# A spectral mixing and state-space kernel on one core: the first input tile in one transfer, a fourth staging buffer, and one constant that borrows another's place

## The chip, the cores and the metric

The kernel runs on one core of a Trainium2 chip. The metric is the device time of the whole program in microseconds; lower is better. The engines are named as in the profile: PE is the matrix multiplier and PEld its weight loads, DVE the vector engine, ACT the scalar (activation) engine, POOL the general one, and SP the engine whose queue issues nearly all transfers.

## The reference

Two independent branches, side by side in the output (2048 x 1024, single precision). Branch A is a Fourier mixing layer written as matrix products, branch B a long convolution with a kernel made from state-space parameters, here with the same length L = 2048 and width D = 512.

```
# branch A: real part of a DFT along the hidden and the sequence axis
a = einsum("bsd,ed->bse", x, dft_hid_re);  b = einsum("bsd,ed->bse", x, dft_hid_im)
yA = einsum("ts,bse->bte", dft_seq_re, a) - einsum("ts,bse->bte", dft_seq_im, b)
# branch B
dt = exp(log_dt);  A = -exp(log_A_real) + 1j*A_imag;  C = (C_real + 1j*C_imag)*dt
K  = 2 * Re( sum_n C[d,n] * exp(A[d,n]*dt[d]*l) )          # [D, L]
yB = irfft( rfft(u, 2L) * rfft(K, 2L) )[:L] + u * D_skip
out = concatenate([yA, yB], -1)
```

## The kernel before

**Branch A** (class `Fnet`) does the sequence transform first. For four column blocks t and the two parts c (cosine, sine) it forms x^T times a 512-column block of the sequence matrix: eight "s" groups of 16 k steps, whose results p go to DRAM. Then four "p" groups of 8 k steps multiply them with the hidden matrix. Each single-precision operand is split into a rounded `hi` (ACT, L212) and a remainder `lo` (DVE, L216), and a product is three matmuls: hi by hi, hi by lo, lo by hi (L333). A k step is four output blocks d of three matmuls each, 128 x 128 by 128 x 512, so twelve; there are 1,920 in all. The stationary x tiles are loaded once, into `x_raw`, four slots of a buffer that branch B uses later (`uk`). The moving tiles (sT, later p) come through four `raw` buffers and three `hi`/`lo` pairs.

A group's four PSUM banks are evacuated by ACT into `y` buffers (`evacuate`, L359) and stored from there by SP (L364 to p, L367 to the output). There are three y buffers (`STAGED`); a y is free again when its store has landed. The last block of the last group uses two of them, one half copied by ACT (L353), the other by DVE (L354).

**Branch B** (class `Ssm`) builds the kernel's taps from tables (DVE, ACT; L575, L584, L591), multiplies them on PE (L771), and runs a two-stage transform: stage one of u (`stage1_u`, L846, with the constant `f1u`) and of the taps (L801, `f1k`), each stored to DRAM (xu, L862; xk); stage two (`product`, L926, with `w2`, loads L899), the product on DVE, and two inverse stages (L961 with `ia`, L1007 in `inverse`, with `ib`, which loads `zl` tiles at L1002). The constants come in two sets (`constants`, L440): f1u, f1k and dskip early, then w2, ia and ib.

**Order.** The order on every engine's queue is made when the program is built. A list scheduler (`Plan`) runs each piece as a generator that asks for an engine with an estimated time (`yield "pe", 0.685, None, 6`: engine, microseconds, urgency, instructions) or waits for an event or a buffer (`Sem`). Of the pieces that could start first, the more urgent one is taken, and its instructions go to the engine's queue at that point; the engine then works strictly in that order. Branch A's matmuls have the lowest rank on PE, so they fill what branch B leaves. The number of y buffers enters as `self.ys = Sem(STAGED)`.

**The start.** The first x tile is loaded in two transfers: the first 128 columns alone (`load_x0`, L247), then the other 384 (`load_x1`, L259). The first sT tile leaves at the same time through ACT's queue (L296). While these travel, PE multiplies zeros (`warm`, L232: seven matmuls, which are 14 instructions in the profile); one more zero matmul stands behind the first three real matmuls.

Of the kernel before, what the change touches and what calls it, by code (L numbers as in the profile page):

```python
# [8 lines left out]
F32 = mybir.dt.float32  # L9
# [47 lines left out]
class Sem:  # L57


    def __init__(self, n):  # L60
        self.free, self.waiting = [0.0] * n, []
# [109 lines left out]
def act(cols):  # L171
    return 0.09 + cols * 0.00085


def dve(cols, rate=1.0):
    return (62 + cols / rate) / 960


def load(kb):
    return max(0.55, kb / 330)  # L180


class Fnet:
# [40 lines left out]

    def warm(self):

        yield "pe", 3.1, None, 28
        self.zeros(7)

    def zeros(self, n):  # L230
        for _ in range(n):
# [11 lines left out]

    def load_x0(self, raw):

        yield "dma", load(64)
        self.nc.sync.dma_start(raw[:, :128], self.xin[0, :, :128])  # L247
        self.x[0] = self.still(0)
        yield "act", act(128)
        self.nc.scalar.activation(self.x[0][0][:, :128], raw[:, :128], AF.Copy)  # L250
        yield "dve", dve(128)
        self.nc.vector.tensor_tensor(self.x[0][1][:, :128], raw[:, :128], self.x[0][0][:, :128].bitcast(F32),
                                     op=OP.subtract)
        self.plan.set(self.x0_ev)

    def load_x1(self, b, raw, n):
        cols = slice(0 if n else 128, DM)
        yield "dma", load(256)
        self.nc.sync.dma_start(raw[:, cols], self.xin[n, :, cols])  # L259
        if n:  # L260
            self.x[n] = self.still(n)
        else:
            yield self.hi_ev
        yield from self.split(*(a[:, cols] for a in self.x[n]), raw[:, cols])
        self.plan.set(self.x_ev[n])
        self.x_left -= 1
        if not self.x_left:
            self.plan.put(b.uks)
# [42 lines left out]
    def matmuls(self):  # L311
        nc = self.nc
        for g in self.groups:
            still = (self.x, self.x_ev) if g[0] == "s" else (self.w, self.w_ev)
            items, acc = self.items[g], []
            for batch in [[i] for i in items[:-BATCH]] + [items[-BATCH:]]:
                for d in range(4):
                    if batch[0][3] == 0:
                        yield self.acc
                        acc.append(self.psum.tile([128, DM], F32, name="acc"))  # L320
                    for i in batch:
                        k = i[3]
                        yield self.m_ev[i]
                        yield still[1][k] if k or d or g != self.groups[0] else self.x0_ev
                        (shi, slo), (mhi, mlo) = still[0][k], self.m[i]
                        first = i == self.items[self.groups[0]][0] and not d
                        yield "pe", 0.685, None, 10 if first else 6
                        cols = slice(128 * d, 128 * d + 128)
                        three = (shi, mhi), (shi, mlo), (slo, mhi)
                        if still[1][k] is self.x_ev[0] and not d:  # L330
                            three = three[::2] + three[1:2]
                        for n, (l, r) in enumerate(three):
                            nc.tensor.matmul(acc[d], l[:, cols], r, start=k == 0 and n == 0,  # L333
                                             stop=k == len(items) - 1 and n == 2)
                        if first:
                            self.zeros(1)
                        if d == 3:
                            self.plan.put(self.ss)
                            self.split_ahead -= 1
                            if i[:3] == ("s", 3, 1) and k < 8:  # L340
                                self.plan.set(self.x_free[k])
                    if batch[-1] is items[-1]:
                        self.plan.spawn(self.evacuate(g, d, acc[d]), -1)
# [54 lines left out]
class Ssm:  # L398


    def __init__(self, tc, ctx, plan, nd, ldt, dsk, uG, f1u, f1k, w2, ia, ib, out):
        self.tc, self.nc, self.plan = tc, tc.nc, plan
        self.nd, self.ldt, self.uG, self.out = nd, ldt, uG, out
        self.const = ctx.enter_context(tc.tile_pool(name="b_const", bufs=1))
        self.fps = ctx.enter_context(tc.tile_pool(name="b_fps", bufs=1, space=PSUM))
        dram = ctx.enter_context(tc.tile_pool(name="b_dram", bufs=1, space=DRAM))
        self.xu = dram.tile([64, 2, 32, DM], F32, name="xu")
        self.xk, self.zs = (dram.tile([4, 64, 2, 32, PART], F32, name=n) for n in ("xk", "zs"))
        self.dt_dram = dram.tile([128, 4], F32, name="dt_dram")
        self.par_dram = dram.tile([128, 4, DM - FIRST], F32, name="par_dram")  # L410
        first = ("f1u", f1u), ("f1k", f1k), ("dskip", dsk)
        second = ("w2", w2), ("ia", ia), ("ib", ib)
        self.cst = [[(n, self.const.tile([128, *a.shape[1:]], F32, name=n), a) for n, a in s] for s in (first, second)]
        self.halfpi = self.const.tile([128, 1], F32, name="halfpi")
        self.slots, self.fs, self.one = [0, 1], Sem(2), Sem(1)
        self.t1s, self.t2s, self.css = Sem(2), Sem(1), Sem(2)
        self.kss, self.res, self.xks = Sem(1), Sem(1), Sem(1)
        self.waiting, self.taps_left, self.pars = [], 16, Sem(1)
        self.sets, self.set_ev = {}, [Event(), Event()]
        self.const_ev, self.const2_ev, self.xu_ev = Event(), Event(), Event()  # L420
        self.xk_ev, self.zs_ev = [Event() for _ in range(4)], [Event() for _ in range(4)]

    def set_buffers(self, i, pool):
# [436 lines left out]
    def store_u(self, x, m, sem):  # L860
        yield "dma", load(512)
        self.nc.sync.dma_start(self.xu.rearrange("s c l d -> (s c) l d")[:, 2 * m:2 * m + 2], x)  # L862
        self.plan.put(sem)
        self.uleft -= 1
        if not self.uleft:
            self.plan.put(self.sets[0].zls)
            self.plan.set(self.xu_ev)

# [127 lines left out]
    def inverse(self, b, h, i, n):  # L996

        nc = self.nc
        z = b.pool.tile([128, n, PART], F32, name="zl", bufs=b.n)
        yield "dma", load(64 * n)  # L1000
        for o in range(0, n, 8):
            nc.sync.dma_start(z[:, o:o + 8], self.zs[h].rearrange("s c l d -> (s c) l d")[:, n * i + o:n * i + o + 8])  # L1002
        (k, ps), = yield from self.banks(1)
        yield "pe", 0.1 + 0.1025 * n, None, 4 * n + 1
        for w in range(n // 2):
            for y in range(2):
                nc.tensor.matmul(ps[64 * y:64 * y + 64, w // 4, PART * (w % 4):PART * (w % 4) + PART],  # L1007
                                 self.ib[:, n * i + 2 * w + y], z[:, 2 * w + y], start=True, stop=True,
                                 tile_position=(0, 64 * y))
        o = n * i // 2  # L1010
        for w in range(0, n // 2, 4):
            yield "act", act(512)
            nc.scalar.activation(z[:, w:w + 4], ps[:, w // 4].rearrange("p (w d) -> p w d", w=4), AF.Copy)
        self.give(k)
        yield "dma", load(32 * n)
        nc.sync.dma_start(self.out[:, o:o + n // 2, PART * h:PART * h + PART], z[:, :n // 2])
        self.plan.put(b.zls)


CHUNK, FIRST = 32, 128  # L1020
RAWS, DEPTH, STAGED, AHEAD = 4, 3, 3, 3
BATCH = 2


# [70 lines left out]
```

## Time and profile before

| | before |
|---|---|
| timed runs, us | 590.11, 591.39, 592.93 (median 591.39) |
| profiled execution, us | 589.94 |
| its span, first to last instruction, us | 588.1 |
| PE, DVE, ACT busy, us | 581.5, 494.3, 381.0 |
| granted PE clock | 1.00 |
| data moved, MB | 125.84 |

Busy time of PE is the time in which at least one matmul is under way; matmuls overlap, so a busy PE can still be slower than it could be. The time of the profiled execution is 1.84 us longer than its span. In timeline rows the columns are start, duration, engine, line, operation and tiles; idle time before the row and what ended it stand in brackets.

### The profile page before, as it was taken

The page shows a single profiled execution, that of the slowest core. Times are in us where ns is not written, and L with a number is a line of the kernel's source. Part 1 is how long each engine was busy: PE and PEld are TensorE (multiplying, and loading weights), DVE is VectorE, ACT ScalarE, POOL GpSimd, SP SyncE. Part 2 cuts the span into 40 slices and gives each one's busy share as a digit, 9 for nine tenths or more (in the row PEclk, how much of TensorE's full clock was granted, in tenths as well). Part 3 has the DMA queues.
Part 4 walks back from the last instruction along what each step waited for, and adds up shares of the span by engine and source line. Part 5 has one row for each costly group of instructions (what it writes and reads, how often), then busy time and mean ns, then how long its engine had stood idle before and what let it go on. Part 6 is the DMA issues. An engine that isn't in the chain of part 4 may idle for free.

```text
span 588.1 us, 14925 instructions
## 1 busy us (share of the span) xinstructions
PE 581.5 (99%) x5968; PEld 441.9 (75%) x5968; DVE 494.3 (84%) x883; ACT 381.0 (65%) x745; POOL 4.8 (1%) x12
## 2 busy tenths in 40 slices
PE   9999999999999999999999999999999999999997
PEld 7767668778778767877787778777877777777785
DVE  6986989999999999999999999999999944254320
ACT  5789884946676767758584866678755536264532
POOL 0000000000000000000000000000000000000000
PEclk9999999999999999999999999999999999999999
DMA  7999996363494369446768594568798845998574
GB/s 264 324 356 320 350 334 220 98 198 79 118 270 111 93 178 265 136 128 167 231 204 244 152 276 129 150 169 258 237 289 215 256 111 163 316 325 266 158 260 144
DMA packets 141238, 125.84 MB, mean 214 GB/s; under 512 B 46192, under 2 KB 106352, under 8 KB 140912
## 3 DMA queue, kind: packets, MB, share of 16 engines
q1 hardware_dynamic: 140880, 124.48, 69.8%
q8 instruction: 47, 0.77, 0.6%
q10 hardware_dynamic: 288, 0.39, 0.2%
q14 instruction: 23, 0.19, 0.1%
HBM read 82.12 MB, written 42.73 MB: 212 GB/s over the span
## 4 chain that ended last, share of the span: by engine, by line
PE 69%; DVE 14%; DMA 7%; ACT 4%; issue 3%; SPq 2%; DVEq 0%; ACTq 0%
PE acc L333 52%; PE f L926 5%; PE f L771 4%; DVE prod L575 4%; DVE lo L216 3%; PE f L961 3%; PE f L1007 3%; DVE t L584 2%; DMA xt<-xk 2%; PE f L801 2%; DMA raw<-in_sT 2%; SPq L899 1%; DMA uk<-in_x 1%; DMA xu<-z 1%; DMA cs<-in_ldt 1%
## 5 line engine op out<-in xcount | busy, mean ns | idle before, releaser
L333 PE MATMUL acc<-hi,x_hi 128*128 128x512 f32 x640 | 257.5, 402 | 0.5 <-ACT x_hi L212 0.2
L333 PE MATMUL acc<-lo,x_hi 128*128 128x512 f32 x640 | 250.0, 391 | 0.2 <-DVE lo L216 0.2
L333 PE MATMUL acc<-hi,x_lo 128*128 128x512 f32 x640 | 249.8, 390 | 0.1
L575 DVE TENSOR_TENSOR prod<-t,cs 128x1024 f32<-128x1024 f32 (+4 forms) x192 | 163.9, 870 | 3.5 <-ACT t L713 1.4
L216 DVE TENSOR_TENSOR lo<-raw,hi 128x512 fp32r<-128x512 f32 x160 | 109.1, 686 | 61.7 <-ACT hi L212 61.7
L333 PEld LDWEIGHTS acc<-hi,x_hi 128*128 128x128 f32 x640 | 120.2, 188 | 48.7 <-issue 20.8
L212 ACT ACTIVATE hi<-raw 128x512 fp32r<-128x512 f32 x160 | 100.2, 628 | 82.3 <-PE acc L333 63.5
L333 PEld LDWEIGHTS acc<-hi,x_lo 128*128 128x128 f32 x640 | 120.3, 188 | 26.5 <-DVE x_lo L216 0.5
L333 PEld LDWEIGHTS acc<-lo,x_hi 128*128 128x128 f32 x640 | 120.4, 188 | 23.8 <-DVE lo L216 0.8
L584 DVE TENSOR_TENSOR t<-prod 128x512 f32<-128x512 f32 (+4 forms) x192 | 94.1, 512 | 1.0
L591 ACT ACTIVATE square<-t 128x256 f32<-128x256 f32 (+1 forms) x64 | 36.7, 573 | 30.0 <-DVE t L584 28.1
L359 ACT ACTIVATE y<-acc 128x512 f32<-128x512 f32 x47 | 27.9, 597 | 11.7 <-PE acc L333 8.4
L771 PEld LDWEIGHTS f<-t,t 128*32 128x32 f32 x2048 | 29.5, 110 | 6.4 <-issue 3.8
L938 ACT ACTIVATE uk<-f 128x1024 f32<-128x1024 f32 x32 | 31.9, 1013 | 3.7 <-PE f L926 3.7
L926 PE MATMUL f<-xt,w 64*32 64x256 f32 x1024 | 31.9, 379 | 0.6 <-DMA xt<-xk 0.5
L771 PE MATMUL f<-t,t 128*32 128x64 f32 x2048 | 32.2, 220 | 0.3 <-issue 0.3
L941 DVE TENSOR_TENSOR z<-uk 128x512 f32<-128x512 f32 x32 | 22.0, 687 | 6.8 <-ACT uk L938 6.8
L926 PEld LDWEIGHTS f<-xt,w 64*32 64x32 f32 x1024 | 18.6, 106 | 11.9 <-issue 3.7
L650 ACT ACTIVATE cs<-cs 128x352 f32<-128x352 f32 x32 | 16.1, 538 | 14.2 <-DVE cs L645 14.2
L604 DVE TENSOR_TENSOR t<-square 128x128 f32<-128x128 f32 (+1 forms) x64 | 24.7, 386 | 0.0
L976 ACT ACTIVATE z<-f 128x512 f32<-128x512 f32 x32 | 17.5, 596 | 10.2 <-PE f L771 5.1
L598 DVE SCALAR_TENSOR_TENSOR t<-t 128x128 f32<-128x128 f32 (+2 forms) x48 | 22.4, 466 | 0.3
(81 smaller groups left out, 411.5 us busy)
## 6 DMA issues: line engine op xcount, KB each, us to landing
raw<-in_sT SPq DMA_DIRECT2D x127, 256.0 KB, 3.7
p<-y SPq DMA_DIRECT2D x32, 256.0 KB, 4.2
xt<-xu SPq DMA_DIRECT2D x32, 256.0 KB, 4.8
xk<-xk_sb SPq DMA_DIRECT2D x32, 256.0 KB, 4.0
xt<-xk SPq DMA_DIRECT2D x32, 256.0 KB, 5.4
zs<-z SPq DMA_DIRECT2D x32, 256.0 KB, 3.7
zl<-zs SPq DMA_DIRECT2D x16, 512.0 KB, 6.4
raw<-p SPq DMA_DIRECT2D x32, 256.0 KB, 4.0
```

The lines of the kernel that those rows point to most:

```text
L212: self.nc.scalar.activation(hi, src, AF.Copy)
L216: self.nc.vector.tensor_tensor(lo, src, hi.bitcast(F32), op=OP.subtract)
L333: nc.tensor.matmul(acc[d], l[:, cols], r, start=k == 0 and n == 0, stop=k == len(items) - 1 and n == 2)
L359: self.nc.scalar.activation(y, ps, AF.Copy, scale=-1.0 if g[2] == 1 else 1.0)
L575: self.nc.vector.tensor_tensor(p.rearrange("p k d c m -> p k (d c) m"), src.rearrange("p d c l -> p (d c) l")[:, None, :, rows].to_broadca ...
L584: self.nc.vector.tensor_tensor(dst[:, :, :, rows], p[:, 0], p[:, 1, :, ::-1], op=OP.add)
L591: self.nc.scalar.activation(sq, t[:, :, :, m // 2:m], AF.Square)
L598: self.nc.vector.scalar_tensor_tensor(t[:, :, 1, m:2 * m:2], t[:, :, 0, m // 2:m], 2.0, t[:, :, 1, m // 2:m], op0=OP.mult, op1=OP.mult)
L604: self.nc.vector.tensor_tensor(t[:, :, 0, m:2 * m:2], box[0][:, :, 0], box[0][:, :, 1], op=OP.subtract)
L771: nc.tensor.matmul(ps[32 * j:32 * j + 32, i], t1[:, d, c], t2[:, d, c], start=c == 0, stop=c == 1, tile_position=(0, 32 * j))
L926: nc.tensor.matmul(both[:, :, c], self.w2[rows, 2 * q + r, xx, 32 * c:32 * c + 32], xt[rows, r, xx], start=True, stop=True, tile_position= ...
L938: a.activation(uk[:, r].rearrange("p g n c d -> p g (n c d)"), p, AF.Copy)
```

## The change

Three things change. (1) The first x tile comes in one transfer of 256 KB; `load_x1` no longer issues one for it, but ACT and DVE still split the first 128 columns ahead of the others. The scheduler is told 440 KB for this one transfer. (2) All eight zero matmuls stand ahead of the first real one, none behind it. (3) There are four y buffers instead of three. `f1u` has no place of its own: it lies in the first 128 columns of `ib`, and `ib` is loaded only when the last store of u's first stage has been scheduled (`const3_ev`); `inverse` waits for that before it loads its `zl`.

```diff
     def warm(self):
-        yield "pe", 3.1, None, 28
-        self.zeros(7)
+        yield "pe", 3.5, None, 32
+        self.zeros(8)
...
     def load_x0(self, raw):
-        yield "dma", load(64)
-        self.nc.sync.dma_start(raw[:, :128], self.xin[0, :, :128])
+        yield "dma", load(440)
+        self.nc.sync.dma_start(raw, self.xin[0])
         self.x[0] = self.still(0)
...
     def load_x1(self, b, raw, n):
         cols = slice(0 if n else 128, DM)
-        yield "dma", load(256)
-        self.nc.sync.dma_start(raw[:, cols], self.xin[n, :, cols])
         if n:
+            yield "dma", load(256)
+            self.nc.sync.dma_start(raw, self.xin[n])
             self.x[n] = self.still(n)
         else:
             yield self.hi_ev
...
                         (shi, slo), (mhi, mlo) = still[0][k], self.m[i]
-                        first = i == self.items[self.groups[0]][0] and not d
-                        yield "pe", 0.685, None, 10 if first else 6
+                        yield "pe", 0.685, None, 6
...
-                        if first:
-                            self.zeros(1)
...
-        first = ("f1u", f1u), ("f1k", f1k), ("dskip", dsk)
-        second = ("w2", w2), ("ia", ia), ("ib", ib)
-        self.cst = [[(n, self.const.tile([128, *a.shape[1:]], F32, name=n), a) for n, a in s] for s in (first, second)]
+        constants = ("f1u", f1u), ("f1k", f1k), ("dskip", dsk), ("w2", w2), ("ia", ia), ("ib", ib)
+        t = {n: self.const.tile([128, *a.shape[1:]], F32, name=n) for n, a in constants[1:]}
+        t["f1u"] = t["ib"][:, :2].rearrange("p l y -> p (l y)")
+        cst = [(n, t[n], a) for n, a in constants]
+        self.cst = cst[:3], cst[3:5], cst[5:]
...
         self.uleft -= 1
         if not self.uleft:
+            self.plan.spawn(self.constants(2, self.const3_ev), 3)
             self.plan.put(self.sets[0].zls)
             self.plan.set(self.xu_ev)
...
         z = b.pool.tile([128, n, PART], F32, name="zl", bufs=b.n)
+        yield self.const3_ev
         yield "dma", load(64 * n)
...
-RAWS, DEPTH, STAGED, AHEAD = 4, 3, 3, 3
+RAWS, DEPTH, STAGED, AHEAD = 4, 3, 4, 3
```

More of the change, by code (lines that the diff above doesn't have):

```diff
@@ L419, in __init__ @@
         self.sets, self.set_ev = {}, [Event(), Event()]
-        self.const_ev, self.const2_ev, self.xu_ev = Event(), Event(), Event()
+        self.const_ev, self.const2_ev, self.const3_ev, self.xu_ev = Event(), Event(), Event(), Event()
         self.xk_ev, self.zs_ev = [Event() for _ in range(4)], [Event() for _ in range(4)]
```

## The prediction

> **What bounds the kernel now.** I read the page first (busy shares, slices), then stretches of time, then who waits for whom on the matmul engine, then the chain of waits, and last the timeline where the change acts.
>
> ```profile
> span 588.1 us, 14925 instructions
> PE 581.5 (99%) x5968; PEld 441.9 (75%) x5968; DVE 494.3 (84%) x883; ACT 381.0 (65%) x745; POOL 4.8 (1%) x12
> PE   9999999999999999999999999999999999999997
> ...
> 0.00:10.00 10.00, 8.57 (x33) 6.88 (x34) 4.83 (x13) 5.06 (x9) 0.20 (x4) 1.00 0.74 247
> 80.00:90.00 10.00, 10.00 (x164) 7.69 (x161) 8.55 (x18) 8.21 (x18) 0.00 (x0) 1.00 0.94 354
> 500.00:588.00 88.00, 83.83 (x784) 63.83 (x782) 30.20 (x46) 35.46 (x56) 0.00 (x0) 1.00 0.80 245
> ```
>
> The matmul engine (PE) has work in every slice but the last. In a row of the stretches the columns are length, then busy time of PE, weight loads (PEld), DVE, ACT and POOL, the granted clock, the DMA share and GB/s. PE is idle 588.1 - 581.5 = 6.6 us of the span: 1.4 us in the first 10 us and 4.2 us in the last 88 us. The clock is granted in full. Between 80 and 90 us the transfers are at 0.94 and PE still has no hole.
>
> A busy PE can hide a slow pace, so I look at the pace, at the end of the chain, and at PE's waits (total, times, longest).
>
> ```profile
> 125.64 21.30 PE acc L333 x93
> 575.96 8.40 PE acc L333 x36
> ...
> PE f L926 <- DMA xt<-xk: 0.5, 1, 0.5
> ...
> PEld f L926 <- ACT t L716: 1.4, 4, 0.4
> PEld acc L333 <- ACT y L359: 1.2, 3, 0.6
> PEld acc L333 <- ACT x_hi L212: 1.2, 2, 0.8
> PEld acc L333 <- DVE lo L216: 0.8, 2, 0.6
> ```
>
> Undisturbed, 93 matmuls take 21.30 us, 0.229 us each; 1,920 of L333 at that pace are 440 us, and the second branch's matmuls fill nearly all the rest. No wait of PE for another engine in the steady part exceeds 0.5 us. The last 36 matmuls run 8.4 us without a break after the last one of the second branch, so that branch could end some microseconds later before anything moves. The kernel is bound by PE's work, and the change takes none of it away: it has the same 1,920 matmuls, the same second branch, the same eight zero matmuls.
>
> **The change, part 1: the first x tile, and the filler.**
>
> ```profile
> 0.74 0.40 SPq L247 DMA_DIRECT2D uk<-in_x  x1
> 0.74 0.40 ACTq L296 DMA_DIRECT2D raw<-in_sT  x1
> 1.05 3.36 PE L232 MATMUL acc<-y 128*128 128x128 f32 x14 [1.05 <-DVE y L206]
> 1.19 0.89 SPq L259 DMA_DIRECT2D uk<-in_x  x2
> 3.60 0.31 ACT L250 ACTIVATE x_hi<-uk 128x128 fp32r<-128x128 f32 x1 [1.14 <-DMA uk<-in_x]
> 3.85 0.63 ACT L212 ACTIVATE hi<-raw 128x512 fp32r<-128x512 f32 x1
> 4.51 0.69 DVE L216 TENSOR_TENSOR lo<-raw,hi 128x512 fp32r<-128x512 f32 x1 [0.28 <-ACT hi L212]
> 4.53 0.79 PE L333 MATMUL acc<-hi,x_hi 128*128 128x512 f32 x1
> 5.25 1.04 ACT L212 ACTIVATE x_hi<-uk 128x512 fp32r<-128x512 f32 x2 [0.77 <-DMA uk<-in_x]
> 5.76 0.38 PE L232 MATMUL acc<-y 128*128 128x128 f32 x2
> 5.91 1.16 DVE L216 TENSOR_TENSOR x_lo<-uk,x_hi 128x512 fp32r<-128x512 f32 x2 [0.71 <-ACT x_hi L212]
> 6.35 0.50 PE L333 MATMUL acc<-hi,x_hi 128*128 128x512 f32 x1 [0.20 <-ACT x_hi L212]
> 7.13 0.50 PE L333 MATMUL acc<-hi,x_lo 128*128 128x512 f32 x1
> ...
> raw<-in_sT ACTq DMA_DIRECT2D x1, 256.0 KB, 3.1
> uk<-in_x SPq DMA_DIRECT2D x15, 256.0 KB, 4.9
> uk<-in_x SPq DMA_DIRECT2D x1, 192.0 KB, 3.2
> uk<-in_x SPq DMA_DIRECT2D x1, 64.0 KB, 2.8
> ```
>
> Now the 64 KB piece lands at 0.74 + 2.8 = 3.54 and releases ACT at 3.60; sT lands at 0.74 + 3.1 = 3.84; the 192 KB piece, issued at 1.19, at 4.39. After the change x and sT, 256 KB each, leave together at 0.74. Those are the 512 KB that are here by 4.39, so I let both land at 4.39. The bounds are the other 256 KB transfers, 3.84 (the 3.1 us of ACT's queue) and 5.64 (the median 4.9 us of the fifteen others). 4.39 is an inference from equal bytes.
>
> The steps from 4.39, by the gaps between the rows above: L250 starts at 4.45, the split of sT 0.25 later at 4.70 and ends at 5.33; the first real matmul starts at 5.38 instead of 4.53. DVE's lo follows 0.66 behind the start of hi, from 5.36 to 6.05. But the second and third matmul groups wait for something else. ACT's order has tile x1 ahead of the rest of x0: it sits idle 0.77 us until x1 lands, at 5.25. With the same bytes ahead of it, x1 lands at the same time, and ACT is free at about 5.30. So the pair of ACT starts 0.05 late, the next group at 6.40 instead of 6.35, and the x_lo pair on DVE starts about 5.97 instead of 5.91, which puts the row at 7.13 to 7.19. From there PE runs at its steady pace. The 0.85 us by which the first group is late is absorbed by the idle 0.77 us of ACT and the hole from 6.14 to 6.35. **Net +0.06 us.** At 5.64 for x0 the reserve is used up and 1.25 us come through; if x1 gains the 0.45 us of the removed issue (two issues take 0.89), it is -0.45 us.
>
> The filler: two more instructions of L232 ahead at 3.36/14 = 0.24 each reach 4.41 + 0.48 = 4.89, still before 5.38, so PE waits for data, not for the filler. The removed pair lay in PE's hole before 6.35. Cost 0 both times. A hole is left where the filler was; its only price could be the clock. The first real matmul takes 0.79 us and those at 6.35 and 7.13 take 0.50, so the array wakes up in these microseconds, some 3.5 us after the filler's start at 1.05. The Trainium skill, "TensorE: Matmul & The Clock Gate", section "A second HAM failure mode: psum-queue depth-cycling", warns that short idle pauses between groups of matmuls can make the clock fall back and pay the warm-up again. By that page's window of about 3.4 us at half rate the sum would be about 1.7 us more (an estimate). The trace, with a clock of 1.00 in the first stretch and pauses like the one before 6.35 in it, does not show such a fall; it is a rival below, priced from rows.
>
> **Part 2: the fourth y buffer.** A group's four evacuations (L359) need a y each, and the fourth must wait until the first has been stored. PE feels that where the next group's fourth matmul set wants the bank.
>
> ```profile
> 118.68 0.59 ACT L359 ACTIVATE y<-acc 128x512 f32<-128x512 f32 x1
> 118.76 0.39 PE L333 MATMUL acc<-hi,x_lo 128*128 128x512 f32 x1
> 119.32 0.50 PE L333 MATMUL acc<-hi,x_hi 128*128 128x512 f32 x1 [0.18 <-ACT y L359]
> ...
> 467.46 0.19 PEld L333 LDWEIGHTS acc<-hi,x_hi 128*128 128x128 f32 x1 [0.38 <-ACT y L359]
> ...
> p<-y SPq DMA_DIRECT2D x32, 256.0 KB, 4.2
> ```
>
> At 119.32 PE is (119.32 - 118.76) - 0.229 = 0.33 us behind its pace. At 467.46 the weight load was 0.38 us idle, but PE itself shows no idle time; counting a third of that gives 0.1 us. All such waits of weight loads are 1.2 us in three places, which is the most that this can give directly. **I take -0.4 us**, bounds 0 and -1.2. What is late next: the order on the other engines, since earlier evacuations put the stores earlier in SP's queue. The group ends where no PE wait is seen gain nothing: there the matmuls of the second branch already cover the wait.
>
> **Part 3: f1u inside ib, ib loaded late.**
>
> ```profile
> 76.41 0.43 SPq L440 DMA_DIRECT2D ib<-in_ib  x1
> ...
> L862 SPq DMA_DIRECT2D xu<-zl x11: 327/422/541, 32.8 to 90.2; - x11
> ...
> L1002 SPq DMA_DIRECT2D zl<-zs x16: 326/424/549, 293.6 to 563.4; - x16
> ```
>
> The 1 MB goes from 76.4 us to behind the last store of u's first stage, which is issued at 90.2 us, so 14 us later or a little more. The new wait (before the zl load) is first met at 293.6 us, with about 190 us to spare: cost 0. The load's own wait on SP is for matmuls that have then been done, and raw loads queue behind it as they do now: PE has 10.00 of 10.00 busy from 80 to 90 us, just after that same load. Cost 0; taking it away at 76 us gives PE nothing either, since PE had no hole there. Without that cover a transfer behind 1 MB would be late by its time on the engines, 1 MB at the 354 GB/s of that stretch, 3 us.
>
> **The sum.** +0.06 + 0 - 0.4 + 0 = -0.35 us. The order of all engines is written out by a list scheduler, so three changed requests can reorder everything after the first evacuations. I cannot work that out and take 0 for it; the rivals hold its two signs. The profiled run took 589.94 us (span 588.1 and 1.84 outside it) and the three timed ones 590.11, 591.39 and 592.93. The middle of the four is 590.75, and I count from there: **590.4 us**. 0.5%, or 2.95 us, is about what a measurement of this kernel can tell from no change.
>
> **The rivals.**
>
> *The new order loosens PE's waits.* With a free y the scheduler need not spend second-branch matmuls on covering the store, and can place them where operands are ready. The waits of weight loads for producers in the rows above sum to 1.4 + 1.2 + 1.2 + 0.8 = 4.6 us; all of them gone from the 590.75 gives 586.1, three quarters 587.3. Against it: most of each is hidden, as at 467.46. Chance 0.24 for more than 0.5%.
>
> *SP's in-order queue gets the stores at a worse place* (the other side).
>
> ```profile
> SPq L364 <- ACT y L359: 12.4, 12, 4.7
> SPq L367 <- ACT y L359: 12.1, 10, 3.3
> ```
>
> SP already waits 24.5 us in 22 places for an evacuation while raw loads stand behind the store. With a fourth buffer the fourth store is no longer held back, so it comes up ahead of raw loads that now go first. A wait averages 1.1 us. It reaches PE only if the raw tiles behind have less than that in reserve; a k step of 12 matmuls is 2.75 us. If at each of the 11 changes of group PE lost what it lost at 119.32, that is 11 x 0.33 = 3.6 us: 590.4 + 3.6 = 594.0. For it: between 80 and 90 us transfers are at 0.94; against: PE has no hole there. Chance 0.25 for more than 0.5%.
>
> *The clock falls in the pause left by the filler.* If waking up again took the 3.5 us from the filler's start to the first real matmul, at 0.79 us a matmul instead of 0.50, PE would lose 3.5 x (1 - 0.50/0.79) = 1.3 us: 591.7. Chance 0.04, inside 0.5%.
>
> *The fourth buffer does not do what it says*, since the bank or the copy is what comes last anyway: 590.8. Chance 0.11, inside 0.5%.
>
> **How the numbers follow.** Forecast 0.36; with the last two rivals 0.51 lie within 0.5%, 0.24 below, 0.25 above. The range for 8 in 10 takes in the bounds of part 1 and 2 and most of both order rivals: 586.8 to 594.2. The likeliest case's own range, since signs are mixed, is 589.1 to 592.1: 590.4 with -0.45 and the further -0.8 of part 2 below it, and +1.25 and the +0.4 of part 2 above.
>
> **What would show it.** Right: L250 starts near 4.4 to 4.5 us, the first L333 matmul near 5.4, but the steady pace still from about 7.2; no idle PE before an L333 matmul released by L359; PE's busy time within 1 us of 581.5; ib's issue between 90 and 105 us and zl loads not waiting for it. Wrong: x1 landing late with x0 (steady pace from 8 us or later), waits of PE for raw splits at group changes, a larger stretch of the second branch after L333's last matmul, or more than 10 us idle on PE.

## The result, and the profile after

| | runs | median us (lowest to highest) | ratio to before, 95% interval |
|---|---|---|---|
| before | 10 | 590.96 (589.18 to 592.97) | 1 |
| changed | 10 | 587.02 (586.18 to 588.52) | 0.9935 [0.9916, 0.9953] |
| changed, measured again later | 8 | 586.62 (586.26 to 587.59) | 0.9946 [0.9926, 0.9967] |

The change saves 3.9 us, or 0.65% (0.47% to 0.84% by the interval); in the second measurement it saves 3.2 us against 589.80 for before. The forecast was 590.4, no change by the bound of 0.5%. The profiled execution of the changed kernel, at 588.50 us, is one of its slowest. The head of its page, PE's waits, two stretches, and two groups of transfers:

```profile
span 586.7 us, 14914 instructions
PE 580.0 (99%) x5968; PEld 443.1 (76%) x5968; DVE 494.6 (84%) x883; ACT 381.1 (65%) x745; POOL 3.6 (1%) x12
...
PE f L770 <- ACT uk L938: 1.3, 1, 1.3
PE acc L232 <- DVE y L206: 1.1, 1, 1.1
PE acc L332 <- ACT hi L212: 0.6, 1, 0.6
...
0.00:10.00 10.00, 8.38 (x27) 7.08 (x28) 5.10 (x15) 5.27 (x9) 0.20 (x4) 1.00 0.78 264
500.00:588.00 88.00, 82.94 (x807) 62.32 (x805) 29.54 (x45) 36.79 (x59) 0.00 (x0) 1.00 0.81 246
...
L439 SPq DMA_DIRECT2D ib<-in_ib x1: 502/502/502, 99.1 to 99.1; - x1
L1003 SPq DMA_DIRECT2D zl<-zs x16: 327/424/477, 297.0 to 566.1; - x16
```

The lines have moved: L332 is the main matmul, L356 the evacuation, L770 the taps, L1008 the last stage. Past the start PE has a single wait, 1.3 us, for ACT's copy out of a second-branch bank; the wait for y (L356) is gone from PE's list, ib is issued at 99.1 us, and zl is first loaded at 297.0.

This execution lost 1.7 us against before in its first 12 us. Timeline of the changed kernel:

```profile
4.51 0.31 ACT L250 ACTIVATE x_hi<-uk 128x128 fp32r<-128x128 f32 x1 [2.07 <-DMA uk<-in_x]
5.25 1.03 ACT L212 ACTIVATE x_hi<-uk 128x512 fp32r<-128x512 f32 x2
5.40 0.79 PE L332 MATMUL acc<-hi,x_hi 128*128 128x512 f32 x1 [0.57 <-ACT hi L212]
...
8.12 0.63 PE L332 MATMUL acc<-hi,x_hi 128*128 128x512 f32 x1
...
9.83 0.63 PE L332 MATMUL acc<-lo,x_hi 128*128 128x512 f32 x1
10.26 0.49 PE L332 MATMUL acc<-hi,x_lo 128*128 128x512 f32 x1
10.58 0.39 PE L332 MATMUL acc<-hi,x_hi 128*128 128x512 f32 x1
```

The first real matmul starts at 5.40, and then matmuls start 0.43 us apart instead of 0.23 until 10.26: the array runs at half its pace for eleven matmuls, although the granted clock of this stretch reads 1.00. The twentieth real matmul starts at 12.18 us, against 10.48 before.

To see what is left, I went through the starts of all matmuls of each trace and added up, past 12 us, what each gap exceeds the undisturbed pace (0.227 us between main matmuls, a block's usual duration for the second branch). Before: 4.5 us; changed: 1.5 us. So the steady part gained 3.0 us and the start lost 1.7 in this execution, which is close to the difference of the spans, 588.1 - 586.7 = 1.4.

Before, six places lose more than 0.3 us, 3.7 us together: 0.34 us each in front of main matmuls at 119 and 276, 1.2 us in the second-branch block at 213, and 0.6 to 0.7 us in each of those at 285, 344 and 513. Past 12 us the changed kernel has one such place, 1.4 us at 178.

### The profile page after: what moved, and what is told of

Same layout as the page of the kernel before. It is cut to its first block, busy times and chain, and to the rows that moved or that the text cites. A ratio compares the mean times of both kernels' runs of the same rounds, so it can differ in the third digit from the quotient of the medians.

```text
span 586.7 us, 14914 instructions
## 1 busy us (share of the span) xinstructions
PE 580.0 (99%) x5968; PEld 443.1 (76%) x5968; DVE 494.6 (84%) x883; ACT 381.1 (65%) x745; POOL 3.6 (1%) x12
## 4 chain that ended last, share of the span: by engine, by line
PE 83%; DVE 9%; ACT 4%; issue 2%; DMA 2%; SPq 0%; ACTq 0%
PE acc L332 64%; PE f L926 5%; PE f L770 4%; DVE prod L574 3%; PE f L961 3%; PE f L1008 3%; PE f L845 2%; PE f L800 2%; DVE t L583 2%; DVE lo L216 2%; ACT hi L212 1%; DMA par<-par_dram 1%; DMA uk<-in_x 1%; DVE t L603 1%; ACT L631 1%
## 5 line engine op out<-in xcount | busy, mean ns | idle before, releaser
L332 PE MATMUL acc<-hi,x_hi 128*128 128x512 f32 x640 | 257.6, 403 | 0.6 <-ACT hi L212 0.6
L332 PE MATMUL acc<-lo,x_hi 128*128 128x512 f32 x640 | 250.8, 392 | 0.0
L332 PE MATMUL acc<-hi,x_lo 128*128 128x512 f32 x640 | 250.1, 391 | 0.0
L332 PEld LDWEIGHTS acc<-hi,x_hi 128*128 128x128 f32 x640 | 120.6, 188 | 47.9 <-issue 20.8
L332 PEld LDWEIGHTS acc<-hi,x_lo 128*128 128x128 f32 x640 | 120.7, 189 | 26.2
L332 PEld LDWEIGHTS acc<-lo,x_hi 128*128 128x128 f32 x640 | 120.7, 189 | 23.5 <-DVE lo L216 0.2
L583 DVE TENSOR_TENSOR t<-prod 128x512 f32<-128x512 f32 (+4 forms) x192 | 95.6, 517 | 1.1
L356 ACT ACTIVATE y<-acc 128x512 f32<-128x512 f32 x47 | 27.8, 596 | 11.0 <-PE acc L332 10.8
L770 PEld LDWEIGHTS f<-t,t 128*32 128x32 f32 x2048 | 29.3, 110 | 7.3 <-issue 4.1
L770 PE MATMUL f<-t,t 128*32 128x64 f32 x2048 | 31.9, 220 | 1.3 <-ACT uk L938 1.3
```

The costliest lines, as they stand in the source:

```text
L356: self.nc.scalar.activation(y, ps, AF.Copy, scale=-1.0 if g[2] == 1 else 1.0)
L583: self.nc.vector.tensor_tensor(dst[:, :, :, rows], p[:, 0], p[:, 1, :, ::-1], op=OP.add)
L770: nc.tensor.matmul(ps[32 * j:32 * j + 32, i], t1[:, d, c], t2[:, d, c], start=c == 0, stop=c == 1, tile_position=(0, 32 * j))
```

## The experiments

The order on every queue is fixed when the program is built, so two kernels can be compared in two respects: the order, and what the instructions wait for. Theories after the result: *order* (the scheduler, given four buffers, wrote an order in which PE is served in time), *buffer* (evacuations no longer wait for a store), *start* (the gain is in the first 10 us), and for the start's loss the *clock*. Stall is the sum just described, in the one profiled execution; two executions of one order can differ in it by about a microsecond, as before and e1 do (4.5 and 5.7).

| kernel | order written for | real y | median us | ratio, 95% interval | stall us |
|---|---|---|---|---|---|
| before | 3 | 3 | 589.8 to 591.0 | 1 | 4.5 |
| e1_start | 3, as before | 3 | 590.11 | 1.0001 [0.9985, 1.0017] | 5.7 |
| e6_before_order_four_real | 3, as before | 4 | 590.47 | 1.0005 [0.9990, 1.0020] | 5.1 |
| e3_late_ib | 3, ib late | 3 | 594.97 | 1.0075 [1.0052, 1.0097] | 8.6 |
| e4_late_ib_four_real | 3, as e3 | 4 | 595.94 | 1.0092 [1.0071, 1.0114] | 10.1 |
| e12_three_lat34 | 3, other estimate | 3 | 595.31 | 1.0094 [1.0065, 1.0123] | 12.4 |
| e2_y_only | 4, ib late | 4 | 586.50 | 0.9928 [0.9906, 0.9950] | 1.6 |
| e8_more_filler | 4, as changed | 4 | 586.58 | 0.9931 [0.9913, 0.9950] | 1.8 |
| e5_three_real | 4, as changed | 3 | 590.01 | 0.9999 [0.9983, 1.0016] | 4.1 |
| e7_four_early_ib | 4, ib early | 4 | 596.22 | 1.0090 [1.0067, 1.0112] | 5.1 |
| e10_four_lat32 | 4, other estimate | 4 | 587.08 | 0.9954 [0.9937, 0.9971] | 1.3 |
| e11_four_lat34 | 4, other estimate | 4 | 600.03 | 1.0173 [1.0141, 1.0205] | 10.0 |

**The parts of the change.** e1_start takes over only the transfer and the filler; every other queue entry stands as before. e2_y_only takes over the rest.

```diff
 # e1_start: before, with warm, load_x0, load_x1 and matmuls of the changed kernel
 # e2_y_only: changed, with those four as before
-RAWS, DEPTH, STAGED, AHEAD = 4, 3, 3, 3
+RAWS, DEPTH, STAGED, AHEAD = 4, 3, 4, 3     # e2_y_only only, with f1u in ib and ib late
```

> Only part 1: the first x tile in one transfer, all eight zero matmuls ahead, three y buffers, constants as before; every queue keeps the order of before. Order theory (the gain of 3.9 us comes from the order that the scheduler wrote with four y buffers): 591 as before, at most 2.3 us more where the PE clock wakes late. Start theory (the gain is made in the first 10 us): 587 to 588.

> Only parts 2 and 3: four y buffers, f1u inside ib, ib late, with the start of before; past the start every queue has the order of the changed kernel. Order theory: 586 to 587, and nearer to 586 if the filler of before keeps the clock awake. Start theory: 591.

The start theory falls: e1 is at 1.0001. The whole gain is in e2, and e2's executions lie within 0.7 us (586.22 to 586.91).

**ib late, with three buffers.**

```diff
-RAWS, DEPTH, STAGED, AHEAD = 4, 3, 4, 3     # e2_y_only
+RAWS, DEPTH, STAGED, AHEAD = 4, 3, 3, 3     # e3_late_ib
```

> Only part 3: f1u inside ib and ib late, with three y buffers and the start of before. The scheduler writes an order of its own again (about a sixth of PE's instructions move). If the gain needs the fourth buffer: 591, the stalls of about 4 us in the steady part stay. If the late ib alone makes it: 587. Any other order as good as chance: between 588 and 594.

It is 0.75% slower than before, so moving one load, with the wait that goes with it, made the scheduler write an order that costs 4.8 us. One of its two large stalls (the other, 2.32 us at 286.23, is of the same kind), in ACT's and PE's timeline:

```profile
224.22 0.62 ACT L593 ACTIVATE square<-t 128x512 f32<-128x512 f32 x1
224.85 1.28 ACT L632 ACT_TABLE_LOAD   x1
226.15 0.50 ACT L632 ACTIVATE seed<-seed 128x352 f32<-128x352 f32 x1
226.55 0.58 ACT L359 ACTIVATE y<-acc 128x512 f32<-128x512 f32 x1
...
227.18 0.50 PE L333 MATMUL acc<-hi,x_hi 128*128 128x512 f32 x1 [2.13 <-ACT y L359]
```

PE is idle 2.13 us for an evacuation. But ACT is not: it works without a pause and has an activation with its table load ahead of the copy. The profile gives y as the releaser, and the reason is a place in ACT's queue.

**The same order with a fourth real buffer.** e4 keeps e3's order on all queues; the scheduler goes on counting three.

```diff
-... self.ys = Sem(4), Sem(RAWS), Sem(DEPTH), Sem(STAGED)
+... self.ys = Sem(4), Sem(RAWS), Sem(DEPTH), Sem(3)        # STAGED = 4 still sizes the pool
```

> The order of e3_late_ib on every queue (written for three y buffers, ib late), with four real y buffers behind it. In e3_late_ib PE waited 6.5 us in five places for the copy into y. If the stores' waits are what cost it: 595.0 - 4.7 to 595.0 - 6.5, so 588.5 to 590.3. If the order itself is bad: 594 to 595.

```profile
225.65 1.28 ACT L632 ACT_TABLE_LOAD   x1
226.95 0.50 ACT L632 ACTIVATE seed<-seed 128x352 f32<-128x352 f32 x1
227.35 0.58 ACT L359 ACTIVATE y<-acc 128x512 f32<-128x512 f32 x1
...
227.98 0.50 PE L333 MATMUL acc<-hi,x_hi 128*128 128x512 f32 x1 [2.13 <-ACT y L359]
```

The buffer theory falls here: the same 2.13 us with a free buffer at hand. In this order a buffer that it does not count on gains nothing. e6 says the same for the order of before; there f1u lies in ia's place and the 64 KB of ia are loaded at the end of u's first stage, outside the plan.

> The order of before on every queue, with four real y buffers; room is made by putting f1u in ia's place, and the 64 KB of ia are loaded behind the last store of u's first stage. Order and buffer together (an order written for three buffers leaves little for the fourth to do; PE waits for y were 1.2 us): 589 to 590, 0.4 to 1.2 below before. Buffer alone: 586 to 587. Neither: 590.2.

It is at 1.0005. None of ACT's copies waits for a store any more, so the buffer does its work, but the wait of PE that the prediction priced is still there:

```profile
118.79 0.58 ACT L813 ACTIVATE xk_sb<-f 128x512 f32<-128x512 f32 x1
119.26 0.59 ACT L359 ACTIVATE y<-acc 128x512 f32<-128x512 f32 x1
119.90 0.50 PE L333 MATMUL acc<-hi,x_hi 128*128 128x512 f32 x1 [0.17 <-ACT y L359]
```

**The changed order with three real buffers.**

```diff
-        y = self.pool.tile([128, DM], F32, name="y", bufs=STAGED)
+        y = self.pool.tile([128, DM], F32, name="y", bufs=3)      # all three places; self.ys stays at 4
```

> The changed kernel with its order on every queue, but with only three y buffers behind it (the scheduler still plans with four). Order theory: 587 to 588, at most 1.2 us more than the changed kernel. Buffer theory (the evacuations that need not wait for a store make the gain): back to 590 to 591, with PE waits released by the copy into y at the changes of group.

The order theory in its simple form falls as well: the good order with three buffers is no better than before. Here the store itself is waited for, and this time ACT stands idle in front of the copy (timeline, and the waits of PE):

```profile
282.26 0.60 ACT L356 ACTIVATE y<-acc 128x512 f32<-128x512 f32 x1 [2.40 <-DMA p<-y]
282.91 0.50 PE L332 MATMUL acc<-hi,x_hi 128*128 128x512 f32 x1 [1.42 <-ACT y L356]
...
PE acc L332 <- ACT y L356: 1.4, 1, 1.4
PE f L1008 <- DMA zl<-zs: 0.8, 1, 0.8
```

In the changed kernel none of ACT's 47 copies waits for a store; in e5 three do, 4.9 us together. So order and buffer are needed together: the order places copies early, and the buffer lets them run there. PE's other waits in e5 (0.8 us for zl, 0.6 us for POOL's work on ks) are not traced to the missing buffer.

**Is it the number of buffers, or this one order?** e7 plans with four, but with ib early (f1u in ia's place as in e6). e10, e11 and e12 change only what the scheduler believes a transfer takes.

```diff
-HOP, RESULT, LATENCY = 0.3, 0.15, 3.3
+HOP, RESULT, LATENCY = 0.3, 0.15, 3.2     # e10 on e2_y_only; 3.4 in e11 on e2_y_only and in e12 on before
```

> Four y buffers, planned and real, but ib loaded early as before (f1u lies in ia's place, ia is loaded behind the last store of u's first stage); start of before. The scheduler writes yet another order. If four buffers planned and real make the gain whatever the order: 586 to 588. If the changed kernel's order was luck: anywhere from 586 to 594.

> Four y buffers, f1u in ib, ib late, start of before; the scheduler believes a transfer takes 3.2 us instead of 3.3, which does nothing but write another order. Luck theory (the gain belongs to this one order, not to the fourth buffer): the time moves by 1 to 8 us, most likely up, 588 to 594. Buffer theory (four buffers let the scheduler write better orders in general): 586 to 588.

> As the run before, with 3.4 us: luck theory 588 to 594, buffer theory 586 to 588.

> The kernel before with three y buffers, the scheduler believing 3.4 us instead of 3.3. Luck theory: anywhere from 587 to 595, above or below the 590.2 of before. Buffer theory: 590 to 595, and not below the two runs with four buffers.

Four buffers give 586.5, 587.1, 596.2 and 600.0; three give 590, 595.0 and 595.3. An estimate 0.1 us up costs 13.5 us with four buffers and 5.5 us with three. The runs at 595.3, 596.2 and 600.0 lie above what I had expected under any theory. In e7 and e11 the end is what fails: the second branch ends last and PE waits for its loads after the main matmuls are done. PE's waits of e7, then of e11:

```profile
PE f L1011 <- DMA zl<-zs: 4.5, 1, 4.5
...
PE f L1011 <- DMA zl<-zs: 5.0, 2, 4.3
PE acc L333 <- DVE lo L216: 2.7, 2, 2.1
```

The gain belongs to the order that was found with four buffers, and to one near it (in e10 760 of PE's 5,968 instructions stand in another place than in e2, in e11 2,266), not to four buffers as such. Why the scheduler hits a good order at 3.2 and 3.3 and a bad one at 3.4 stays open.

**The clock.** e8 lets PE's filler last until the first real matmul; e9 is the changed kernel again.

```diff
-        self.zeros(8)
+        self.zeros(10)      # e8_more_filler; the plan's numbers stay
```

> The changed kernel with ten zero matmuls ahead instead of eight, so that PE's filler reaches the first real matmul at about 5.4 us; all queues otherwise the same. Clock theory (the pause between filler and first real matmul lets the clock wake some 3 us late in part of the executions): all executions at 586.2 to 586.9, median 586.5 against 587.0 and a spread of 2.3 us. Otherwise: median 587.0 with the same spread, or 0.1 us more.

> The changed kernel once more, beside the next three on the same chip. Clock theory: median 586.5 to 587.3, with part of the executions 1.5 to 2.3 us above the lowest; a profile of a slow one shows the first real matmuls at half pace beyond 7 us. Against it: a spread below 1 us, as with more filler.

e8: 585.96 to 587.01, median 586.58. e9: 586.26 to 587.59, median 586.62, and its profiled execution (586.45 us) wakes early:

```profile
6.16 0.63 PE L332 MATMUL acc<-lo,x_hi 128*128 128x512 f32 x1
6.59 0.44 PE L332 MATMUL acc<-hi,x_hi 128*128 128x512 f32 x1
6.87 0.40 PE L332 MATMUL acc<-lo,x_hi 128*128 128x512 f32 x1
```

The same code reaches full pace at about 6.7 us here and at 10.3 us in the first profile. The twentieth real matmul starts at 10.32 us instead of 12.18, 1.86 of the 2.05 us between those two executions; 0.26 us of it is a first real matmul that starts earlier, at 5.14, and 1.6 us is the late waking. e1 and e5 have the same start and wake early too, at about 7.0 and 5.9 us. PE stood idle in front of the first real matmul for 0.57 us in the execution that woke late, and for 0.31 (e9), 0.29 (e1) and 0.08 us (e5) in the others. That a late waking happens is shown; that the longer pause causes it and more filler cures it is not, since only one profile shows it and in this second measurement the changed kernel had no execution above 587.6 either. With e2_y_only at 586.50 and e8 at 586.58, no version is measurably better than the changed kernel.

## Why the range held and the size was missed, point by point

The measured 587.02 lies inside the range, 0.2 us from its lower end (the second measurement, 586.62, lies 0.2 us below that end), and 3.4 us below the sum. The range held because it took in both signs of the order, not because the sum saw the gain. That the order was a good one is luck as far as the prediction goes: four buffers with one estimate 0.1 us higher gave 600.0, far above the range.

*What bounds the kernel: right.* In every profile PE's last matmul starts at about 579 us (578.9 to 579.5) plus the stall of the table and what the start lost, except where the second branch ends last (e7, e11). There was nothing to win but stalls. PE's busy time fell to 580.0, 1.5 us and not within 1 us as the signs asked, since part of the stalls counts as busy, as in the block at 213 shown below.

*Part 1, net +0.06 us: right as far as the runs can tell.* L250 was put at 4.45 and came at 4.51, the first real matmul at 5.38 and came at 5.40, the ACT pair at 5.30 and came at 5.25. e1 is at 1.0001, with an interval of about 1 us either way. In the first profile the steady pace came only at 10.3 us, not at 7.2. With an early clock the twentieth real matmul of e9 starts at 10.32, 0.16 us earlier than before.

*The clock rival, chance 0.04 and 1.3 us: the price was near (1.6 to 1.7 us), and it can come up in single executions.* It came up in the first profile, and it did not set the result: the median is 3.9 us below before. The filler had ended before the data came, and PE stood idle 0.57 us. The run shows a late waking, not a fall from full pace: the filler before it ran at the slow pace too, 0.21 us from start to start, against 0.11 us for the pair of zero instructions at 5.76 in the kernel before. The rule of the Trainium skill that I set beside it ("TensorE: Matmul & The Clock Gate", section "A second HAM failure mode: psum-queue depth-cycling") and the trace agree on the half pace, 0.43 us against 0.23, and not on the fall.

*Part 3, cost 0: right for the load itself* (issued at 99.1, no PE wait for it), *wrong as an edit*: with three buffers, putting it there rewrites the order and costs 4.8 us (e3).

*Part 2, -0.4 us, is the reading that failed.* I took the copy at 118.68 as late because no y was free. ACT's row carries no idle time in front of it; it was late because of what stands ahead in ACT's queue, and e6 with a free buffer has the same stall. The row ahead of that copy, and what ACT waited for before its copies, in the kernel before:

```profile
118.20 0.58 ACT L810 ACTIVATE xk_sb<-f 128x512 f32<-128x512 f32 x1
...
DMA p<-y: 2.0, 2
DMA out_ya<-y: 1.1, 1
```

Three copies did wait for a store, at 170.08, 466.81 and 524.65. Only the second is followed by a late weight load, the one at 467.46, which was read rightly; it cost PE about 0.1 us. By its interval e6 leaves room for -0.6 to +1.2 us, so the term itself is not refuted; its reason at 119.32 is.

*The order, taken as 0, is the mis-sized term.* It measured -3.7 us together with the buffer that it counts on (e2), and nothing without it (e5). I saw that three requests could reorder everything and put the two signs into rivals of 0.24 and 0.25. The first of them came true, though mostly not by its list: the four rows of weight-load waits still sum to 2.8 us of 4.6 in the changed kernel, with that for L716 unchanged at 1.4 us. What went, besides the two places in front of main matmuls, were waits like these of the kernel before, where a second-branch block stood on PE before its bank or its tile was there:

```profile
213.37 1.00 ACT L938 ACTIVATE uk<-f 128x1024 f32<-128x1024 f32 x1
214.42 0.31 PEld L801 LDWEIGHTS f<-ks,f1k 32*128 32x128 f32 x8 [0.92 <-ACT uk L938]
...
513.13 1.24 PE L926 MATMUL f<-xt,w 64*32 64x256 f32 x33 [0.51 <-DMA xt<-xk]
```

PE's busy time hid part of them: the block at 213 takes 3.1 us instead of 1.9, and the list of PE's waits shows none of it. So the reading that no wait of PE in the steady part exceeds 0.5 us left out losses that a busy PE hides. For the blocks at 285 and 344 the trace names no other engine, and why they went stays open.

The other rival's condition came true without its price. SP's waits for the copy rose from 24.5 us in 22 places to 32.1 us in 33, and past the start PE's list shows no wait for a raw split:

```profile
SPq L361 <- ACT y L356: 19.6, 20, 2.7
SPq L364 <- ACT y L356: 12.5, 13, 3.1
```

## What to carry to other kernels

Where the queues are written by a scheduler, any edit of its inputs is first a new order. Its size should be taken from orders, by moving an estimate a little, before a gain is put down to the edit: here 0.1 us in one estimate moved the time by up to 13.5 us. A wait that the profile puts down to a copy is a wait for a buffer only if the copying engine stands idle in front of it, and a store ends that idle time. To learn whether a buffer matters, vary the number that the scheduler counts and the number that exists apart from each other.

## What the runs showed that I had not expected

The spread within one kernel may follow its order too. e2's six executions lie within 0.7 us and those of the changed kernel within 2.3 and 1.3 us, those of before within 3.3 to 4.3 us in each set; but e10, also a good order, spreads over 3.3 us. In e1, which has the order of before, PE lost time to loads that the trace of before does not show:

```profile
PE f L1004 <- DMA zl<-zs: 0.8, 2, 0.4
```

It fits that transfers which land just in time make the spread, but no run varied that alone.
